# POOL made to wait for the DVE operations planned as sharing its SBUF port, and a weight conversion taken through PSUM, in a fused attention and gated-MLP kernel

## The chip, the cores and the metric

The kernel runs on one core of one Trainium2 chip. The metric is the device time of one execution in microseconds (us). In this text PE is TensorE, DVE is VectorE, ACT is ScalarE, POOL is GpSimd, and SP is the engine whose queue issues most DMAs.

## The reference

An attention block between 512 tokens and 32 states for each of 8 batches and 8 heads (D = 64) gives 4352 rows of 512 values. A gated MLP with 2048 hidden units follows.

```python
scores = scale * x @ state.T          # softmax over the states
xread  = softmax(scores) @ state      # (B, H, 512, 64)
sread  = softmax(scale * state @ x.T) @ x   # (B, H, 32, 64)
y = concatenate([xread, sread], axis=2)     # to (4352, 512)
h = y @ w_in                          # 512 x 2048
g = h * cos(h)
out = g @ w_out                       # 2048 x 512, float32
```

Attention inputs are float32; w_in and w_out come as float64 and are made float32 in the kernel.

## The kernel before

**Tiles.** The token rows are worked on batch by batch, 16 tiles of 128 hidden units each. For a batch, "products" multiplies the states with w_in (state products, result sw_all), so that a hidden tile is one product of the attention weights aT_all with sw_all. A gate follows: ACT rounds (q_all), DVE subtracts, ACT takes a sine, DVE multiplies with h and writes g_all. Output products then take g_all with w_out. Batches 0 and 1 are the first pair and use plain products. From batch 2 on two batches share seven-product block schemes (Strassen's kind) for the hidden tiles ("seven_part", with sums on POOL in sw_sums and on DVE in seven_sum and halves) and for the output products (class Product; its sums of g_all are POOL's, and outer_sum gives more on DVE or POOL). Weight blocks for these are written to device memory (blocks_kept) and fetched into a ring. At the end come the state rows.

**Two lists.** Engines work strictly in the order in which instructions are issued to each. first_pair orders the work of batches 0 and 1 (the first list): each Task has an engine, a cost, what it reads and writes, a due step, and a mark "shares" for a DVE operation that the planner takes to share an SBUF port with POOL. Its instructions all have line L44 in the profile. All later work is first recorded on a tape and then ordered by in_order (the second list, line L1870), with the same kind of planning. In both, a planned lock keeps a sharing DVE operation and a POOL operation from overlapping in the plan; in the running kernel nothing enforced this, unless data did. The planned order of one engine is fixed; between two engines only semaphores for data hold.

**Conversion.** convert(i, p) makes float32 of one piece i of float64 weights (18 pieces, the first four of half size) in five steps: "1" and "2" on ACT (high and low words), "b" on DVE (shift left by three, in place), "c" on DVE (sign bit from the raw words, xor), "d" on POOL (adds the low part). CONV gives the order of pieces 4 to 17, CONV_DUE their due steps. PACE turns a due step into a time, NEAR is how long the planner lets a more urgent task hold the engine, ARRIVED says when the first seven loads are taken to have landed.

**Names.** h_pairs[1] is a pair of PSUM banks ("sd00" to "sd11" in the tasks), used by the state products of the first pair and from batch 2 on by hidden tiles. at is another bank pair, for attention. acc is the pair of output accumulators.

Of the kernel before, what the change touches and what calls it, by code (L numbers as in the profile page):

```python
# [11 lines left out]
I32 = mybir.dt.int32  # L12
# [10 lines left out]
def kernel(  # L23
# [11 lines left out]
    class Lane:  # L35
        def __init__(self, name, engine):
            self.name, self.engine = name, engine

        def __getattr__(self, op):
            f = getattr(self.engine, op)  # L40

            def call(*args, **kw):
                if not taping[0]:
                    return f(*args, **kw)  # L44
                tape.append((self.name, op, f, args, kw, burst[0]))
            return call

    class Lanes:
# [44 lines left out]
    TEMPS = 4  # L93
# [144 lines left out]
    def convert(i, p):  # L238
        if not f64:
            return  # L240
        raw, dst = raws[i], loads[i][0]
        bits = dst.bitcast(I32)
        m, w = dst.shape[1:]
        c0 = m * w if i in (2, 3) else 0
        e = low[i % 2][:, c0:c0 + m * w].rearrange("p (m f) -> p m f", m=m)
        e = e.bitcast(I32)
        if p == "1":
            nc.scalar.activation(dst, raw.bitcast(F32)[:, :, :, 1],
                                 func=ACTF.Abs, scale=2.0 ** -112)
        elif p == "2":  # L250
            nc.scalar.activation(e, raw.bitcast(U32)[:, :, :, 0],
                                 func=ACTF.Copy, scale=2.0 ** -29)
        elif p == "b":
            nc.vector.tensor_scalar(bits, bits, 3, None,
                                    op0=ALU.logical_shift_left)
        elif p == "c":
            nc.vector.scalar_tensor_tensor(out=bits, in0=raw[:, :, :, 1],
                                           scalar=-2 ** 31, in1=bits,
                                           op0=ALU.bitwise_and,
                                           op1=ALU.bitwise_xor)  # L260
        else:
            nc.gpsimd.tensor_tensor(bits, bits, e, op=ALU.add)
# [734 lines left out]
    WARM, START_PE = 8, 19.7  # L997
    ARRIVED = (10.0, 11.3, 12.7, 14.0, 16.6, 19.3, 22.0)

# [165 lines left out]
    def first_pair_tasks():  # L1165
# [10 lines left out]
        def dve(n):  # L1176
            return .06 + n * .00108
# [23 lines left out]
        def conversion(i, due):  # L1201
            n = 512 if i < 4 else 1024
            raw, w, e = raw_of(i), weight_of(i), low_of(i)
            if i > (6 if f64 else 4):
                add("sp", .4, lambda: fetch(i), "", raw, due - 3)
            for p, engine, cost, r, wr, sh in (
                    ("1", "act", act(n) + .05, raw, w, False),
                    ("2", "act", act(n) + .05, raw, e, False),
                    ("b", "dve", n * .0007 + .03, w, w, True),
                    ("c", "dve", dve(n), raw + " " + w, w, True),  # L1210
                    ("d", "pool", pool(n), e + " " + w, w, False)):
                add(engine, cost, lambda p=p: convert(i, p), r, wr, due,
                    sh)

        def attention(b, k):
# [26 lines left out]
            for j in range(2 if b == 0 else 0):  # L1242
                add("act", act(512) + .03,
                    lambda j=j: a.exp1(slice(j, j + 1)), f"z{z}{j}",
                    f"z{z}{j}", k + 4)
            m2 = k + 6 if b == 0 else k + 4
            if b == 0:
# [83 lines left out]
        def tile_(t, k):  # L1331
            n = t.b * NF + t.f
            h, z, c = n % 2, t.b % 2, t.f // 4 % 2
            g = names(quads_of[t.row][t.i // QT], t.i % QT)
            add("pe", 1.72, lambda: hidden(t),
                f"sw{c}{t.f % 4 // 2}0 sw{c}{t.f % 4 // 2}1 z{z}0 z{z}1",
                f"h{h} H", k)
            add("act", act(512) - .04, lambda: gate(t), f"h{h}", f"q{h}")
            add("dve", dve(512) - .02, lambda: gate2(t), f"h{h} q{h}", f"q{h}")
            add("act", .63 if n else 1.91, lambda: gate3(t), f"q{h} T",  # L1340
                f"q{h}")
            add("dve", dve(512) - .02, lambda: gate4(t), f"h{h} q{h}", g,
                k + 2)

# [148 lines left out]
        for step, what in (  # L1493
                (1, lambda: attention_late(0, 0)),
                (3, lambda: products(0, 1, 2.5)),
                (3, lambda: add("pe", .4, lambda: states(1, side_banks[0]),
                                "held0", "sd00 sd01", 8.5)),
                (3, lambda: add("act", .53,
                                lambda: states_kept(1, side_banks[0]),
                                "sd00 sd01", "stT1", 5.5)),  # L1500
                (5, lambda: attention(1, 4)),
                (7, lambda: products(0, 2, 4.5)),
                (11, lambda: products(0, 3, 11.5)),
                (13, lambda: products(1, 0, 16)),
                (13, lambda: attention_late(1, 18)),
                (13, lambda: inner(0, a11, 5, temps[0], names(TEMPS), 14.5)),
                (15, lambda: sends(2, a22, 8, 17)),
                (15, lambda: sums_of(SQ, A21, A22, add_, 16, "pool")),
                (16, lambda: products(1, 1, 18.5)),
                (16, lambda: inner(3, matrix(SQ), SQ, temps[1], E, 17)),  # L1510
                (17, lambda: sums_of(A22, SQ, A11, sub_, 16, "pool")),
                (17, lambda: attention(2, 19)),
                (18, lambda: sums_of(A21, A11, A21, sub_, 20, "dve")),
                (20, lambda: products(1, 2, 23)),
                (20, lambda: inner(5, matrix(A21), A21, temps[0],
                                   names(TEMPS), 20)),
                (20, lambda: sends(1, a12, 6, 22)),
                (21, lambda: inner(4, matrix(A22), A22, temps[1], E, 22)),
                (23, lambda: sums_of(SQ, A12, A22, sub_, 23, "dve")),
                (24, lambda: inner(6, matrix(SQ), SQ, temps[0], names(TEMPS),  # L1520
                                   25)),
                (24, lambda: products(1, 3, 31)),
                (25, lambda: attention_late(2, 25)),
                (24, lambda: [add("sp", .4, lambda n=n: fetch_block(n), "B3",
                                  f"ring{n}", 27) for n in range(NB - 1)])):
            at_step[step].append(what)
        t32, t34 = all_tiles[PERIOD], all_tiles[PERIOD + 2]
        for step, what in (
                (26, lambda: outer(0, 2, 0, 0, 26, "dve")),
                (27, lambda: outer(0, 2, 0, 1, 27, "dve")),  # L1530
                (28, lambda: tokens_of_next(32)),
                (28, lambda: products(2, 0, 28)),
                (28, lambda: p5_tasks(30.5)),
                (29, lambda: weight_columns(t32, 30.5)),
                (29, lambda: add("dve", .7, lambda: halves(2, 0), "z00 z01",
                                 "E0", 30, True)),
                (29, lambda: add("dve", .7, lambda: halves(2, 1),
                                 "z00 z01 E0", "E1", 30, True)),
                (30, lambda: seven_tasks(t32, 29.5)),
                (31, lambda: weight_columns(t34, 32)),  # L1540
# [3 lines left out]
        for step, t in enumerate(all_tiles[0:FIRST]):  # L1544
# [3 lines left out]
            if 4 <= step < 4 + NH:  # L1548
                first(step - 4, step - 1)
            for i in range(NH):  # L1550
                if SECOND_AT[i] == step:
                    second(i, step)
        for what in at_step[FIRST]:
# [3 lines left out]
    SECOND_AT = (16, 17, 19, 20, 22, 24, 26, 27)  # L1557
    CONV = (4, 5, 6, 7, 8, 9, 10, 11, 14, 15, 16, 17, 12, 13)
    CONV_DUE = (3, 4.5, 3.5, 6, 6.7, 8.5, 9, 9.5, 12.0, 11, 11.3, 13.7, 12.5, 15.7)
    PACE, NEAR, SEND = 3.4, 0.3, 2.5  # L1560

# [36 lines left out]
    def first_pair():  # L1598
# [20 lines left out]
        lock = 0.0  # L1619
        cold = True  # L1620
        log = []
        while can:
# [17 lines left out]
            if t.engine == "pe":  # L1640
# [3 lines left out]
                if cold and idle > 0:  # L1644
                    warm(idle, acc[0])
            t.what()
            can.remove(t)
            end = at_ + t.cost
            free[t.engine] = end
            log.append((at_, t))  # L1650
# [125 lines left out]
    def works_of(tape):  # L1776
        works, last, at_ = [], {}, 0.0
        wrote, read = {}, defaultdict(list)
        for engine, op, f, args, kw, n in tape:
            aps = [a for a in list(args) + list(kw.values())  # L1780
# [9 lines left out]
            if not (w is not None and w.burst == n  # L1790
# [6 lines left out]
                if op == "matmul" and kw["lhsT"].partition_size() == D:  # L1797
                    w.cost += .3
            w.calls.append((f, args, kw))
            w.cost += cost_of(engine, op, kw, aps)  # L1800
# [22 lines left out]
    def in_order(tape, free):  # L1823
# [15 lines left out]
        while can:  # L1839
# [20 lines left out]
            for u in after[w]:  # L1860
# [4 lines left out]
                if not waiting[u]:  # L1865
                    can.append(u)
        assert len(log) == len(works)
        for w in sorted(log, key=lambda w: w.start):
            for f, args, kw in w.calls:
                f(*args, **kw)  # L1870

# [74 lines left out]
```

## Time and profile before

| what | value |
|---|---|
| median of 3 runs | 730.56 us (727.94 to 731.85) |
| the profiled execution's own time | 726.99 us |
| its span, first to last instruction | 725.2 us |
| mean granted PE clock | 0.992 |
| PE busy | 701.0 us |
| POOL busy | 540.2 us |
| DVE busy | 508.9 us |
| ACT busy | 348.0 us |
| first instruction of the second list on PE | 157.7 us |

How to read it: a busy PE is not PE at its peak, since the ends of matmuls are modelled. The first list takes 157.7 us and holds 127.4 us of PE busy time after the first 20 us; the second takes 567.5 us with 556.5 us of it busy. Most lines belong to helpers (L44 and L1870), so that instructions are told apart by their tiles.

### The profile page before, as it was taken

To read this page: it belongs to the slowest core of one execution; us is meant where nothing else is said; L and a number is where in the kernel's file an instruction comes from. 1 tells how busy PE (TensorE), PEld (TensorE's weight loads), DVE (VectorE), ACT (ScalarE), POOL (GpSimd) and SP (SyncE) were. 2 spreads that over 40 slices of the span, in tenths; PEclk is the share of its full clock that TensorE was granted. 3 is DMA by queue.
4 is the path that set the end of the run, shared out by engine and by line. 5 is a ranking of instruction groups with operands and counts; after the bars stand their busy time and mean duration, and the time that the engine had idled before them with its cause. 6 is when DMAs were issued, how large, how long until landed. Compare 5 with 4: busy or idle time off the path is not lost.

```text
span 725.2 us, 10728 instructions
## 1 busy us (share of the span) xinstructions
PE 701.0 (97%) x3628; PEld 524.1 (72%) x3628; DVE 508.9 (70%) x698; ACT 348.0 (48%) x591; POOL 540.2 (74%) x524
## 2 busy tenths in 40 slices
PE   8898899999979999999999999999999999999997
PEld 4444344477857878787788787878788888888886
DVE  4899879987876687776986567878766476625630
ACT  5689876754543447444634554445634443211100
POOL 1466799578984998898998856998988848896500
PEclk9999999999989999999999999999999999999999
DMA  9966699756436754783258435762366345465851
GB/s 298 294 194 201 190 260 294 190 137 142 142 82 134 205 130 123 149 193 89 78 128 186 118 88 126 153 147 85 114 153 157 89 111 128 110 200 170 224 103 29
DMA packets 204022, 111.34 MB, mean 154 GB/s; under 512 B 149888, under 2 KB 166784, under 8 KB 203968
## 3 DMA queue, kind: packets, MB, share of 16 engines
q1 hardware_dynamic: 202880, 110.14, 58.5%
q8 instruction: 29, 0.48, 0.3%
q10 hardware_dynamic: 960, 0.39, 0.2%
q14 instruction: 25, 0.20, 0.1%
q0 software_dynamic: 128, 0.13, 0.1%
HBM read 87.03 MB, written 23.59 MB: 153 GB/s over the span
## 4 chain that ended last, share of the span: by engine, by line
PE 67%; DVE 3%; issue 1%; ACT 1%; DVEq 0%
PE o L1870 38%; PE h L1870 21%; PE at L1870 8%; DVE g_all L1870 1%; ACT q_all L1870 1%; DVE q_all L1870 0%; DVE h L1870 0%; DVE xT L1870 0%; DVE aS_all L1870 0%; ACT L1870 0%; DVE aT_all L1870 0%; DVE held L1870 0%; DVE sr L1870 0%; DVE m_all L1870 0%; ACT xT L1870 0%
## 5 line engine op out<-in xcount | busy, mean ns | idle before, releaser
L1870 POOL TENSOR_TENSOR g_all<-g_all 128x512 f32<-128x512 f32 x250 | 329.2, 1344 | 29.2 <-PE o L1870 20.0
L1870 PE MATMUL o<-g_all 128*128 128x256 f32 x1448 | 341.3, 381 | 0.0
L1870 PEld LDWEIGHTS o<-g_all 128*128 128x128 f32 x1448 | 273.5, 191 | 46.8 <-issue 5.6
L1870 ACT ACTIVATE q_all<-h 128x1024 int32<-128x1024 f32 (+1 forms) x56 | 54.1, 965 | 108.3 <-PE h L1870 106.8
L1870 DVE TENSOR_TENSOR q_all<-q_all,h 128x1024 f32<-128x1024 int32 (+1 forms) x56 | 64.0, 1142 | 53.4 <-ACT q_all L1870 53.3
L1870 DVE TENSOR_TENSOR g_all<-h,q_all 128x1024 f32<-128x1024 f32 (+1 forms) x56 | 64.1, 1145 | 28.0 <-ACT q_all L1870 25.6
L1870 ACT ACTIVATE q_all<-q_all,halfpi 128x1024 f32<-128x1024 f32 (+1 forms) x56 | 61.1, 1091 | 26.1 <-DVE q_all L1870 25.8
L44 PE MATMUL h<-aT_all,sw_all 128*128 128x512 f32 (+1 forms) x132 | 62.8, 603 | 5.4 <-DVE g_all L44 5.4
L1870 DVE TENSOR_TENSOR g_all<-g_all 128x1024 f32<-128x1024 f32 (+1 forms) x68 | 67.8, 1039 | 0.1
L1870 DVE TENSOR_TENSOR h<-h,sums_all 128x256 f32<-128x256 f32 x94 | 40.1, 427 | 38.1 <-PE h L1870 33.2
L1870 PE MATMUL h<-aS_all,swS_all 128*128 128x256 f32 x188 | 59.0, 396 | 0.0
L1870 PE MATMUL h<-aS_all,sw_all 128*128 128x256 f32 x188 | 56.3, 381 | 2.7 <-DVE h L1870 2.7
L1870 POOL TENSOR_TENSOR swS_all<-sw_all 128x128 f32<-128x128 f32 x46 | 22.3, 486 | 47.6 <-ACT sw_all L1870 47.3
L1870 PE MATMUL h<-aT_all,sw_all 128*128 128x256 f32 x188 | 56.6, 383 | 0.0
L44 PEld LDWEIGHTS h<-aT_all,sw_all 128*128 128x128 f32 x132 | 23.9, 192 | 36.0 <-issue 21.5
L1870 PEld LDWEIGHTS h<-aS_all,swS_all 128*128 128x128 f32 x188 | 33.9, 191 | 21.3 <-POOL g_all L1870 9.2
L44 POOL TENSOR_TENSOR g_all<-g_all 128x512 f32<-128x512 f32 x30 | 42.2, 1426 | 5.1 <-DVE g_all L44 2.4
L44 PE MATMUL o<-g_all 128*128 128x512 f32 (+1 forms) x112 | 43.7, 520 | 0.0
L44 POOL TENSOR_TENSOR w_in<-w_in,aS_all 128x1024 int32<-128x1024 int32 (+1 forms) x10 | 21.4, 2153 | 29.5 <-DVE w_in L44 22.3
L1870 PEld LDWEIGHTS h<-aS_all,sw_all 128*128 128x128 f32 x188 | 35.2, 190 | 9.0 <-DVE h L1870 3.4
L1870 PEld LDWEIGHTS h<-aT_all,sw_all 128*128 128x128 f32 x188 | 35.8, 192 | 5.5 <-DVE g_all L1870 0.6
L1870 DVE SCALAR_TENSOR_TENSOR held<-o,held 128x512 f32<-128x512 f32 x38 | 26.1, 687 | 12.9 <-PE o L1870 12.3
(159 smaller groups left out, 960.2 us busy)
## 6 DMA issues: line engine op xcount, KB each, us to landing
g_all<-blocks_kept SPq DMA_DIRECT2D x206, 256.0 KB, 2.8
blocks_kept<-g_all SPq DMA_DIRECT2D x48, 256.0 KB, 4.1
g_all<-in_moe_w_out_dram SPq DMA_DIRECT2D x8, 1024.0 KB, 5.5
out_dram<-ot SPq DMA_DIRECT2D x128, 64.0 KB, 2.8
g_all<-in_moe_w_in_dram SPq DMA_DIRECT2D x6, 1024.0 KB, 7.2
x_b<-in_x_dram SPq DMA_DIRECT2D x24, 256.0 KB, 4.6
xT<-in_x_dram SPq DMA_DIRECT2D x80, 64.0 KB, 2.8
x_b<-in_x_dram SPq DMA_DIRECT2D x16, 128.0 KB, 4.1
```

Of the source, the lines that this page charges most:

```text
L44: return f(*args, **kw)
L1870: f(*args, **kw)
```

## The change

Three things are changed.

First, a POOL instruction may be given a wait for a DVE instruction. When the planner of either list issues a POOL operation whose planned start is less than 1.0 us after the planned end of the last sharing DVE operation, that POOL operation gets a semaphore dependency on the last DVE instruction issued so far (Lane.behind; it need not be the sharing one).

Second, from piece 4 on step b of the conversion writes to the PSUM pair h_pairs[1] and step c reads it there. The planner then no longer marks b and c as sharing the port, and takes b at DVE's ordinary cost. The first four pieces stay in place in SBUF, and only for them c stays marked.

Third, the first list has new due steps for nearly all its work, two pieces (10 and 11) swapped, and new planner constants.

```diff
 class Lane:
     def __init__(self, name, engine):
         self.name, self.engine = name, engine
+        self.last = self.behind = None
...
+    def issue(self, f, args, kw):
+        made = self.last = f(*args, **kw)
+        if self.behind is not None:
+            tc.add_manual_dep(made.ins, self.behind.ins.name,
+                              mybir.DependencyInfo(
+                                  mybir.DependencyClass.Sync,
+                                  mybir.DependencyReason.DATA),
+                              reason="ports")
+            self.behind = None
...
+    shifted = bits if i < 4 else h_pairs[1].bitcast(I32)
...
     elif p == "b":
-        nc.vector.tensor_scalar(bits, bits, 3, None,
+        nc.vector.tensor_scalar(shifted, bits, 3, None,
                                 op0=ALU.logical_shift_left)
     elif p == "c":
         nc.vector.scalar_tensor_tensor(out=bits, in0=raw[:, :, :, 1],
-                                       scalar=-2 ** 31, in1=bits,
+                                       scalar=-2 ** 31, in1=shifted,
...
-ARRIVED = (10.0, 11.3, 12.7, 14.0, 16.6, 19.3, 22.0)
+ARRIVED = (10.7, 12.1, 13.5, 14.8, 18.2, 20.9, 23.9)
...
+            x, narrow = (w, True) if i < 4 else ("sd00 sd01 sd10 sd11", False)
+            b_cost = n * .0007 + .03 if narrow else dve(n)
...
-                    ("b", "dve", n * .0007 + .03, w, w, True),
-                    ("c", "dve", dve(n), raw + " " + w, w, True),
+                    ("b", "dve", b_cost, w, x, narrow),
+                    ("c", "dve", dve(n), raw + " " + x, w, narrow),
...
-            add("dve", dve(512) - .02, lambda: gate4(t), f"h{h} q{h}", g, k + 2)
+            add("dve", dve(512) - .02, lambda: gate4(t), f"h{h} q{h}", g, k + 7.5)
...
-                (1, lambda: attention_late(0, 0)),
-                (3, lambda: products(0, 1, 2.5)),
+                (1, lambda: attention_late(0, 3.0)),
+                (3, lambda: products(0, 1, 14.0)),
...
-                first(step - 4, step - 1)
+                first(step - 4, step + 13)
...
-                    second(i, step)
+                    second(i, step + 23.0)
...
-CONV = (4, 5, 6, 7, 8, 9, 10, 11, 14, 15, 16, 17, 12, 13)
-CONV_DUE = (3, 4.5, 3.5, 6, 6.7, 8.5, 9, 9.5, 12.0, 11, 11.3, 13.7, 12.5, 15.7)
-PACE, NEAR, SEND = 3.4, 0.3, 2.5
+CONV = (4, 5, 6, 7, 8, 9, 11, 10, 14, 15, 16, 17, 12, 13)
+CONV_DUE = (1.8, 1.5, 2.1, 5.2, 5.3, 5.2, 10.8, 9.3, 9.7, 11.1, 12.6, 13.2, 13.1, 15.7)
+PACE, NEAR, SEND = 3.6, 0.1, 2.5
...
+            if t.engine == "pool" and dve_end is not None:
+                if at_ < dve_end + 1.0:
+                    pool.behind = dve.last
+                dve_end = None
             t.what()
...
+            if t.engine == "dve" and t.shares:
+                dve_end = end
...
         for w in sorted(log, key=lambda w: w.start):
-            for f, args, kw in w.calls:
-                f(*args, **kw)
+            if w.engine == "pool" and dve_end is not None:
+                if w.start < dve_end + 1.0:
+                    pool.behind = dve.last
+                dve_end = None
+            for lane, f, args, kw in w.calls:
+                lane.issue(f, args, kw)
+            if w.engine == "dve" and w.shares:
+                dve_end = w.start + w.cost
```

No instruction is added or taken away on any engine; only targets of b, waits and the order differ.

## The prediction

> **What bounds the kernel now.** I read four views in this order: the waits of PE, the windows with the granted clock, the timeline of one place, and the groups by form. PE is busy for 701.0 of 725.2 us, so time can only come from its few gaps and from slices in which its clock was low. The first instruction of the second list (L1870) stands on PE at 157.7 us; so I asked for PE's waits before it (first fence) and after it (second fence). Columns: waiting engine, tile and line, what ended the wait, total us, times, longest.
>
> ```profile
> PE h L44 <- DVE g_all L44: 5.4, 5, 1.9
> PE at L44 <- ACT xT L44: 4.3, 4, 2.4
> PE at L44 <- DVE g_all L44: 1.5, 1, 1.5
> ```
>
> ```profile
> PE at L1870 <- ACT xT L1870: 4.4, 1, 4.4
> PE h L1870 <- DVE h L1870: 2.7, 4, 0.9
> ```
>
> The first list loses 13.4 us in waits of PE, half of it (6.9) behind gate products on DVE. In the second list one wait of 4.4 us stands out. The windows around it (us, PE busy, PEld, DVE, ACT, POOL, granted PE clock, DMA share, GB/s) show that it costs more than itself: after it the clock is 0.50 and 0.62.
>
> ```profile
> 208.00:213.00 5.00, 0.65 (x3) 0.22 (x2) 5.00 (x3) 0.59 (x2) 3.24 (x4) 0.92 0.22 52
> 213.00:216.00 3.00, 2.96 (x19) 2.45 (x20) 1.63 (x3) 2.16 (x5) 2.20 (x3) 0.50 0.00 0
> 216.00:220.00 4.00, 4.00 (x13) 3.27 (x12) 2.00 (x3) 1.03 (x1) 1.27 (x1) 0.62 0.41 70
> ```
>
> The timeline names the cause. DVE's normalising product of batch 3 (aT_all<-aT_all,xT) takes 7.12 us, during which POOL runs six sums without a gap; ACT's copy of the turned weights waits for that product, and PE's read for the copy.
>
> ```profile
> 205.21 7.12 DVE L1870 TENSOR_TENSOR aT_all<-aT_all,xT 128x1024 f32<-128x1024 f32 x1
> 205.50 2.48 POOL L1870 TENSOR_TENSOR g_all<-g_all 128x512 f32<-128x512 f32 x2
> 207.94 0.45 POOL L1870 TENSOR_TENSOR swS_all<-sw_all 128x128 f32<-128x128 f32 x1
> 208.35 2.48 POOL L1870 TENSOR_TENSOR g_all<-g_all 128x512 f32<-128x512 f32 x2
> 210.79 0.45 POOL L1870 TENSOR_TENSOR swS_all<-swS_all,sw_all 128x128 f32<-128x128 f32 x1
> 212.41 0.58 ACT L1870 COPY xT<-at 128x512 f32<-128x512 f32 x1 [8.77 <-issue]
> 213.04 1.33 PE L1870 MATMUL at<-x_b,xT 128*64 128x128 f32 x10 [4.40 <-ACT xT L1870]
> ```
>
> The groups by form of DVE between 25 and 110 us price the conversion (busy us, then mean ns; TENSOR_SCALAR is its shift b, SCALAR_TENSOR_TENSOR its step c):
>
> ```profile
> L44 DVE SCALAR_TENSOR_TENSOR g_all<-g_all 128x1024 int32<-128x1024 int32 x8 | 10.2, 1281 | 0.1
> L44 DVE TENSOR_SCALAR g_all<-g_all 128x1024 int32<-128x1024 int32 x8 | 9.1, 1143 | 0.4 <-ACT g_all L44 0.4
> L44 DVE SCALAR_TENSOR_TENSOR w_in<-g_all,w_in 128x1024 int32<-128x1024 int32 x6 | 7.1, 1216 | 0.0
> L44 DVE TENSOR_SCALAR w_in<-w_in 128x1024 int32<-128x1024 int32 x6 | 6.1, 1031 | 0.0
> ```
>
> **What the Trainium skill says.** "SBUF — State Buffer", section "Who interferes with whom": a DVE instruction with two SBUF inputs, or in a two-port mode, and a GpSimd instruction that reads SBUF exclude each other for a whole instruction; one with at most one SBUF input outside those modes does not contend. The trace agrees, and adds that a DVE instruction can lose several times running: 7.12 us above, where the timeline has 1.22 for the same number of elements from PSUM. "VectorE: DVE Perf Modes", section "Why PSUM operands drop a tier": an fp32 operation on one tensor that touches PSUM runs one element per cycle. The trace has b at 0.69 us with both sides in SBUF and no case with PSUM. "TensorE: Matmul & The Clock Gate", Part 1: PE's clock is halved after an idle window of about 3.4 us and comes back after as long of work; the trace agrees (0.50 and 0.62 after 4.4 us).
>
> **The change part by part.** The sum is made against the profiled execution's own 726.99 us (span 725.2 and 1.8 around it), which lies 3.6 below the median of 730.56 and under all three runs.
>
> *Waits of POOL, second list.* The built order gives 43 POOL instructions there a wait for a DVE instruction (and 19 in the first list). At the place above, DVE's normalising product now stands ahead of a gate product (before: behind it), and the POOL sum after both waits for the gate product. POOL cannot then hold the port against the normalising product; the latter waits for one running sum at most (1.27). Gone: the wait, 4.4; the clock, 3.00 x (1 - 0.50) + 4.00 x (1 - 0.62) = 3.0. Next late there is ACT, whose sine ends at 203.64, with two copies of 0.58; the read was due at about 208.4, so nothing of that shows. Of the four waits for DVE h, three (0.56 at 231.0, 0.66 at 355.9, 0.65 at 509.4) come after DVE sums that took 1.42 and 1.49 instead of 0.41, or 2.13 instead of 1.22: 1.9. The fourth, 0.87 at 205.4, stands behind a sine that an ACT table load delays; counted at 0. Together -9.3.
>
> *New cost of these waits.* Behind a waiting POOL sum stand all later POOL sums, and for them PE's products and seven-part blocks. Where POOL's sums are done before PE asks, this is free: no wait of PE itself names POOL in the second list, only its weight loads do (9.2 us in 11, each about 0.8, under cover of running matmuls). Bounds: 0, and 43 x 0.45 (the length of a small sum) = 19. I take 1.0, a few waits of some tenths that reach PE. Covered by POOL's lead; if that is gone, see the second rival.
>
> *Changed start of the second list.* The lists meet at other engine positions, so ACT now runs the exponential burst of batch 3 (1.28 table load + 2.6) ahead of two copies of sums that PE's next product needs; before, the copies stood first. PE has about 3.3 us of other work there, against 3.9: +0.6.
>
> *Conversion through PSUM, first list.* Fourteen shifts b write PSUM. The 1024-wide gate product, which touches PSUM, takes 1.22, so b: 14 x 1.22 = 17.1 against 8 x 1.143 + 6 x 1.031 = 15.3 now. Bounds for one b: 0.69 (no loss from PSUM) and 1.30. c stays at 1.22 and loses 0.5 of collisions. DVE: +1.3 (from -6.2 to +2.4). POOL's step d loses its collisions: means 2.63 (x8) and 2.56 (x6) against 2.34 in undisturbed cases, -3.6 of POOL. The bank pair of b and c also serves the state products: each conversion holds it for about 2.4 us, 14 x 2.4 = 34 us of the 85 between 25 and 110, so those products can wait for it; their new places in PE's order allow for that.
>
> *Own due steps.* The same 93 pieces of PE work and as many warm-up matmuls stand in another order; SP's loads move too: an output-weight load passes an input-weight load, and the twelve token loads of batch 3 go in one run, ahead of ring loads and one store. SP issues are short and no PE wait of the second list names a DMA; if that cover went, one landing (2.8) would show. Both halves of the first state product, and so all four first d, now come ahead of the first tile (before: one half), which can cost about 1 at the start. Of the 13.4 us of waits I assume that a good fifth goes, by POOL's relief and the shorter queues ahead of gate products: -3.0; the views give no closer value. Bounds: all waits behind DVE gates gone, -6.9; as many new ones behind the bank pair, +4.
>
> Sum: -9.3 + 1.0 + 0.6 - 3.0 = -10.7, so 716.3 for a profiled run. The median stood 3.6 higher; locks won by chance may be part of that, so I carry half: 718.
>
> **Rivals.** *Only the one long stall goes.* The first list gains nothing (DVE pays for b what POOL gains) and the small waits return elsewhere: -7.4 + 1.6 = -5.8 on the median, 725. For it: DVE is busy 119.4 of the 137.7 us from 20 to 157.7, so it may set the pace there. Against: half of PE's waits there are behind DVE instructions that collisions pushed back.
>
> *POOL becomes the bound* (slower). From 250 to 350 us POOL is busy 89.75 of 100 and about nine of the waits fall there. Headroom 10.25 / 9 = 1.1 us for each: if a wait costs POOL more than that on average, because the DVE instruction named is itself held by ACT or PE (16 of 43 name one that does not share the port), POOL falls behind. At 1.8 us: 9 x 1.8 - 10.25 = 6 us in each of four such stretches, 24 - 10.7 = +13, so 744. Against: POOL's 435.6 of 567.5 in the whole list leaves room to recover.
>
> *The waits do nothing.* If POOL's winning at 205 was chance that the three timed runs mostly lacked, the gain is in the profile alone: 728 to 731. Against: those runs are slower than the profile, not faster.
>
> **Numbers.** My forecast 718: 0.68. Only the long stall: 0.18. Nothing: 0.06. POOL the bound, or the first list's +4 with it: 0.08. A measurement of this kernel can tell about 0.5% (3.7 us) from no change; faster than that 0.85, within it 0.07, slower 0.08. Range 711 (first list at its best) to 727 (the first rival's end).
>
> **What would show it.** Right: no DVE product over 2.5 us in the second list; no PE wait over 2 us and no clock under 0.9 after 160; b near 1.22 and d near 2.34; PE reaches L1870 near 154.7. Wrong: PE waits naming POOL, POOL idle behind DVE gate products for more than 40 us in all, or L1870 later than 157.7.

## The result, and the profile after

| what | before | after |
|---|---|---|
| median, in the session of the prediction | 731.13 us (4 runs) | 719.59 us (4 runs, 718.96 to 720.12) |
| ratio, with its 95% interval | | 0.9852 (0.9825 to 0.9878) |
| the profiled execution's own time | 726.99 us | 719.58 us |
| its span | 725.2 us | 717.8 us |
| first instruction of the second list on PE | 157.70 us | 158.05 us |
| length of the second list | 567.5 us | 559.75 us |

The kernel is faster by about 1.5% in these runs. The two profiled spans differ by 7.4 us, or 1.0%, and all of that lies in the second list; in three later sessions the kernel before had medians of 727.4 to 728.5, against which 719.59 is 1.1 to 1.2% less. In the kernel after, the lines of both lists are recorded in one helper, so all rows have L51. The waits of PE, first from 20 us to its entry into the second list and then in the second list (waiting engine, tile and line, what ended the wait, total us, times, longest):

```profile
PE h L51 <- DVE g_all L51: 6.0, 5, 1.6
PE h L51 <- DVE i_all L51: 1.9, 1, 1.9
PE h L51 <- ACT sw_all L51: 1.3, 1, 1.3
PE at L51 <- ACT xT L51: 0.8, 2, 0.6
PE h L51 <- POOL w_in L51: 0.3, 1, 0.3
```

```profile
PE h L51 <- DVE h L51: 1.7, 3, 1.3
```

The waits of the first fence sum to 10.3 us, as much as before (5.4 + 3.9 + 0.8 + 0.2 in the same stretch). In the second list the wait of 4.4 us for ACT's copy xT is gone, and with it the cold clock, as the granted clock of 0.50 after it is called here. Windows of the kernel after (us, PE busy, PEld, DVE, ACT, POOL, granted PE clock, DMA share, GB/s):

```profile
207.00:212.00 5.00, 5.00 (x36) 4.08 (x35) 3.42 (x5) 2.82 (x4) 5.00 (x8) 1.00 0.36 88
212.00:216.00 4.00, 4.00 (x31) 3.21 (x30) 3.33 (x7) 0.00 (x0) 4.00 (x5) 1.00 0.79 147
216.00:220.00 4.00, 4.00 (x20) 3.40 (x18) 3.92 (x7) 2.22 (x5) 2.62 (x4) 1.00 0.53 123
```

The timeline of the same place shows how far the remedy reaches. The normalising product still takes 4.62 us, not 1.22. Five POOL sums in a row had begun at 195.86; they and two more were planned ahead of the product and have no wait for it. Only the first sum planned after it, which starts at 205.99, has the wait, and that one is for the gate product. PE waits 1.34 us instead of 4.40.

```profile
195.86 6.19 POOL L51 TENSOR_TENSOR g_all<-g_all 128x512 f32<-128x512 f32 x5
...
200.15 4.62 DVE L51 TENSOR_TENSOR aT_all<-aT_all,xT 128x1024 f32<-128x1024 f32 x1
...
204.70 1.21 DVE L51 TENSOR_TENSOR g_all<-h,q_all 128x1024 f32<-128x1024 f32 x1
204.87 1.07 ACT L51 COPY xT<-at 128x512 f32<-128x512 f32 x2 [4.74 <-DVE aT_all L51]
205.84 0.42 DVE L51 TENSOR_TENSOR h<-h,sums_all 128x256 f32<-128x256 f32 x1
205.99 1.27 POOL L51 TENSOR_TENSOR g_all<-g_all 128x512 f32<-128x512 f32 x1 [2.29 <-DVE g_all L51]
...
206.31 0.70 PE L51 MATMUL h<-aS_all,sw_all 128*128 128x256 f32 x2 [1.34 <-DVE h L51]
```

The conversion, groups by form of DVE between 25 and 110 us (busy us, mean ns): b now writes h, a tile in PSUM, c reads it there, and both stay at 1.22 us (the longest of the 28 took 1.228).

```profile
L51 DVE TENSOR_SCALAR h<-g_all 128x1024 int32<-128x1024 int32 x8 | 9.8, 1223 | 0.9 <-ACT g_all L51 0.8
L51 DVE SCALAR_TENSOR_TENSOR g_all<-g_all,h 128x1024 int32<-128x1024 int32 x8 | 9.7, 1216 | 0.1
L51 DVE TENSOR_SCALAR h<-w_in 128x1024 int32<-128x1024 int32 x6 | 7.3, 1220 | 0.1
L51 DVE SCALAR_TENSOR_TENSOR w_in<-g_all,h 128x1024 int32<-128x1024 int32 x6 | 7.3, 1216 | 0.1
```

One place where the first list loses time is its timeline between 29 and 38 us. ACT's rounding, table load and sine for the first gates stand behind a conversion step that waits 2.32 us for a weight load (piece 7 of the weights):

```profile
31.78 1.16 ACT L51 ACTIVATE w_in<-g_all 128x1024 f32<-128x1024 f32 x1 [2.32 <-DMA g_all<-in_moe_w_in_dram]
...
32.84 0.58 ACT L51 ACTIVATE q_all<-h 128x512 int32<-128x512 f32 x1
...
34.46 1.28 ACT L51 ACT_TABLE_LOAD   x1
...
35.76 0.72 ACT L51 ACTIVATE q_all<-q_all,halfpi 128x512 f32<-128x512 f32 x1
...
36.51 0.69 DVE L51 TENSOR_TENSOR g_all<-h,q_all 128x512 f32<-128x512 f32 x1 [1.80 <-ACT q_all L51]
...
37.26 2.07 PE L51 MATMUL h<-aT_all,sw_all 128*128 128x512 f32 x2 [1.59 <-DVE g_all L51]
```

The windows show what follows: PE is busy for 1.09 of the 3 us from 34 to 37, and its clock is then 0.50.

```profile
34.00:37.00 3.00, 1.09 (x16) 0.21 (x16) 1.16 (x4) 2.97 (x4) 2.15 (x1) 0.97 1.01 337
37.00:40.00 3.00, 2.74 (x4) 1.19 (x5) 2.55 (x7) 2.08 (x4) 0.22 (x1) 0.50 1.35 224
```

### The profile page after: what moved, and what is told of

It reads as the page before. It is cut to its first block, busy times and chain, and to the rows that moved or that the text cites. A ratio compares the mean times of both kernels' runs of the same rounds, so it can differ in the third digit from the quotient of the medians.

```text
span 717.8 us, 10738 instructions
## 1 busy us (share of the span) xinstructions
PE 698.7 (97%) x3628; PEld 522.2 (73%) x3628; DVE 491.6 (68%) x698; ACT 348.7 (49%) x591; POOL 508.3 (71%) x524
## 4 chain that ended last, share of the span: by engine, by line
PE 84%; DVE 6%; ACT 4%; DMA 3%; issue 2%; SPq 0%; ACTq 0%; DVEq 0%
PE o L51 45%; PE h L51 30%; PE at L51 9%; DMA g_all<-in_moe_w_in_dram 2%; DVE g_all L51 2%; DVE h L51 1%; ACT q_all L51 1%; DVE w_in L51 1%; DMA x_b<-in_x_dram 1%; DVE q_all L51 1%; ACT sw_all L51 1%; DMA held<-in_state_dram 0%; ACT aS_all L51 0%; SPq L51 0%; DVE i_all L51 0%
## 5 line engine op out<-in xcount | busy, mean ns | idle before, releaser
L51 POOL TENSOR_TENSOR g_all<-g_all 128x512 f32<-128x512 f32 x280 | 351.1, 1281 | 56.2 <-DVE g_all L51 26.3
L51 PE MATMUL o<-g_all 128*128 128x256 f32 (+1 forms) x1560 | 383.4, 391 | 0.0
L51 PEld LDWEIGHTS o<-g_all 128*128 128x128 f32 x1560 | 293.2, 190 | 64.2 <-issue 22.4
L51 ACT ACTIVATE q_all<-h 128x1024 int32<-128x1024 f32 (+1 forms) x88 | 73.2, 832 | 126.8 <-PE h L51 125.4
L51 DVE TENSOR_TENSOR q_all<-q_all,h 128x1024 f32<-128x1024 int32 (+1 forms) x88 | 85.7, 974 | 67.7 <-ACT q_all L51 67.4
L51 PE MATMUL h<-aT_all,sw_all 128*128 128x256 f32 (+1 forms) x320 | 119.4, 474 | 4.7 <-DVE g_all L51 3.4
L51 DVE TENSOR_TENSOR g_all<-h,q_all 128x1024 f32<-128x1024 f32 (+1 forms) x88 | 85.8, 975 | 35.4 <-ACT q_all L51 34.9
L51 ACT ACTIVATE q_all<-q_all,halfpi 128x1024 f32<-128x1024 f32 (+1 forms) x88 | 84.3, 958 | 31.2 <-DVE q_all L51 30.3
L51 PEld LDWEIGHTS h<-aT_all,sw_all 128*128 128x128 f32 x320 | 59.7, 191 | 40.9 <-issue 20.6
L51 DVE TENSOR_TENSOR g_all<-g_all 128x1024 f32<-128x1024 f32 (+1 forms) x78 | 72.7, 970 | 0.1
L51 DVE TENSOR_TENSOR h<-h,sums_all 128x256 f32<-128x256 f32 x96 | 41.1, 428 | 38.4 <-PE h L51 33.5
L51 PE MATMUL h<-aS_all,swS_all 128*128 128x256 f32 x192 | 59.6, 392 | 0.0
L51 PE MATMUL h<-aS_all,sw_all 128*128 128x256 f32 x192 | 57.6, 381 | 1.7 <-DVE h L51 1.7
L51 POOL TENSOR_TENSOR swS_all<-sw_all 128x128 f32<-128x128 f32 x48 | 21.8, 455 | 43.7 <-ACT sw_all L51 24.5
L51 PEld LDWEIGHTS h<-aS_all,swS_all 128*128 128x128 f32 x192 | 34.5, 189 | 20.5 <-POOL g_all L51 8.4
L51 POOL TENSOR_TENSOR w_in<-w_in,aS_all 128x1024 int32<-128x1024 int32 (+1 forms) x10 | 19.3, 1932 | 33.9 <-DVE w_in L51 28.6
L51 PEld LDWEIGHTS h<-aS_all,sw_all 128*128 128x128 f32 x192 | 36.0, 190 | 8.6 <-DVE h L51 2.3
L51 DVE SCALAR_TENSOR_TENSOR held<-o,held 128x512 f32<-128x512 f32 x38 | 26.1, 686 | 13.7 <-PE o L51 12.9
L51 ACT COPY sw_all<-at 128x512 f32<-128x512 f32 x48 | 25.8, 591 | 16.4 <-PE at L51 16.1
L51 ACT COPY o<-o 128x256 f32<-128x256 f32 x26 | 9.4, 360 | 47.1 <-PE o L51 47.0
L51 ACT COPY o<-sums_all 128x256 f32<-128x256 f32 x26 | 9.7, 375 | 44.9 <-PE o L51 44.9
L51 PE MATMUL h<-st_all,w_in 128*128 128x256 f32 x128 | 30.2, 379 | 0.0
```

The costliest lines, as they stand in the source:

```text
L51: made = self.last = f(*args, **kw)
```

## The experiments

The theory to be tested: the second list's gain comes from POOL's waits, not from the new order that the new start of that list brings; the first list gained nothing because the gates on ACT stand behind the late load of piece 7. The rivals: the new order alone does it; POOL's waits or the pass through PSUM ate the first list's gain; the parts add up one by one. The experiments were run in three sessions of four runs each, in which the kernel before has medians of 727.43, 727.60 and 728.45 us; ratios are against those. "Second list at" gives the time at which PE reaches it in the profiled execution of a run.

### No waits, and waits in the second list only

Both keep every order of the changed kernel. The first switches off the assignment to pool.behind in both planners, the second in first_pair alone:

```diff
-                if at_ < dve_end + 1.0:
+                if False and at_ < dve_end + 1.0:
                     pool.behind = dve.last
```

> The changed kernel with none of the POOL waits for DVE, in either list; every engine's order as in the changed kernel. Theory (the waits, not the new order, end the long loss of the SBUF port in the second list): the normalising product of batch 3 again takes 6 to 7 us instead of 4.62, PE waits 4 us or more there, its clock drops after it, and the small waits at 231, 356 and 509 come back; 724 to 728 us. Rival (the new order is enough, since the normalising product now stands ahead of the gate product): no PE wait over 2 us after 160, 718 to 721 us.

Measured: 729.99 us, ratio 1.0023 (1.0003 to 1.0044). The second list starts at 158.55 and is 568.05 us long: the whole gain is gone. The timeline of the run without waits:

```profile
200.64 10.10 DVE L51 TENSOR_TENSOR aT_all<-aT_all,xT 128x1024 f32<-128x1024 f32 x1
...
203.89 2.51 POOL L51 TENSOR_TENSOR g_all<-g_all 128x512 f32<-128x512 f32 x2
...
206.33 0.48 POOL L51 TENSOR_TENSOR swS_all<-sw_all 128x128 f32<-128x128 f32 x1
206.74 2.51 POOL L51 TENSOR_TENSOR g_all<-g_all 128x512 f32<-128x512 f32 x2
209.18 0.48 POOL L51 TENSOR_TENSOR swS_all<-swS_all,sw_all 128x128 f32<-128x128 f32 x1
210.66 1.21 DVE L51 TENSOR_TENSOR g_all<-h,q_all 128x1024 f32<-128x1024 f32 x1
...
212.27 1.22 PE L51 MATMUL h<-aS_all,sw_all 128*128 128x256 f32 x2 [6.81 <-DVE h L51]
```

The product stands for 10.10 us, until POOL's queue has run empty, and the gate product stands behind it, so that PE waits 6.81 us. The new order without waits is worse at this place than the old one (4.40). Its windows have the cold clock again, 0.50 from 212 to 216:

```profile
212.00:216.00 4.00, 3.73 (x9) 3.02 (x10) 2.36 (x4) 1.76 (x4) 2.09 (x3) 0.50 0.00 0
```

> The changed kernel with the POOL waits in the second list only (the 19 of the first list are left out). Theory (the first list is held up by the late load of weight piece 7, not by POOL's waits): the second list is still reached within 1 us of 158.0, 718.5 to 721 us. Rival (POOL's waits in the first list cost the 3 us that were expected as a gain): second list reached at 155 to 156, 716 to 717 us.

Measured: 721.07 us, ratio 0.9903 (0.9870 to 0.9936); second list reached at 158.54 and 559.82 us long. PE's waits in the second list, without POOL's waits and then with them:

```profile
PE h L51 <- DVE h L51: 8.2, 3, 6.8
```

```profile
PE h L51 <- DVE h L51: 1.7, 3, 1.4
```

The two runs issue the same matmuls in the same order. Set side by side, the second list is shorter by 8.2 us: 5.4 at the long wait, 1.9 in the cold clock after it, and 0.3 to 0.4 net at each of the three small ones. The waits do it, the order does not. What they are worth in the first list can't be told from these starts: 158.54 and 158.55 without them, 158.05 with them.

### The kernel before with the waits alone

The parts of the diff that make pool.behind were put into the kernel before, first in both lists, then in the second only; due steps, constants and conversion stayed as before.

> The kernel before with the POOL waits added in both lists and nothing else (old due steps, conversion in SBUF). Theory (the waits alone give the second list's gain): POOL's sums planned after the normalising product of batch 3 wait for it, it takes under 2.5 us although it still stands behind the gate product, no clock drop at 213; second list 559 to 561 us long, in all 721 to 725 us. Rival (the gain is that of the new order, and the waits without it only make POOL stand): PE waits of 2 us or more stay behind the turned weights' copy, 727 to 732 us.

Measured: 720.68 us, ratio 0.9900 (0.9866 to 0.9933); second list at 159.35, 558.9 us long. In the old order, too, the product is at its undisturbed length, and no wait for the copy remains:

```profile
206.53 0.42 DVE L51 TENSOR_TENSOR h<-h,sums_all 128x256 f32<-128x256 f32 x1
206.86 1.21 DVE L51 TENSOR_TENSOR aT_all<-aT_all,xT 128x1024 f32<-128x1024 f32 x1
```

> The kernel before with POOL's waits in the second list only: its own first list, no PSUM conversion, no new due steps. Theory (the second list's waits are the whole gain of the change; the first list of before is as good as that of the changed kernel): second list reached at 157.7 and 558.9 us long, 717.5 to 719.5 us, not slower than the changed kernel. Rival (the old first list brings the second list into an order, or POOL into a lag, that the waits can't mend): 722 to 727 us.

Measured: 720.10 us (718.99 to 721.62), ratio 0.9891 (0.9867 to 0.9914); second list at 159.61, 558.8 us long. The length came as expected, the start 1.9 us later than the 157.70 of the profile before, with the same first list. So two profiles of one first list can differ by about 2 us. Set matmul beside matmul, 1.7 of the 1.9 us arise between 70 and 74 us. In both profiles PE has waited 1.91 us behind a gate product just before; after it the clock stays at 1.00 in the profile of before and falls to a mean of 0.57 in this run:

```profile
70.00:74.00 4.00, 4.00 (x11) 1.71 (x9) 3.93 (x7) 4.00 (x6) 0.10 (x1) 1.00 0.12 45
```

```profile
70.00:74.00 4.00, 4.00 (x7) 1.54 (x5) 3.93 (x7) 3.62 (x5) 0.02 (x1) 0.57 0.17 66
```

The waits alone reach what the whole change reaches, within what can be told apart; in one session, the kernel before with the waits in both lists has 720.68, and the changed kernel with those of the second list 721.07. The rest of the change is worth nothing that these runs can show.

### The conversion in place, with the new order kept

```diff
-        shifted = bits if i < 4 else h_pairs[1].bitcast(I32)
+        shifted = bits
```

The planner still takes b and c as not sharing the port, so nothing keeps them from POOL.

> The changed kernel with step b of pieces 4 to 17 again in place in SBUF and c reading it there; all engine orders and the planner's claims on the bank pair kept. Theory (the pass through PSUM neither makes nor breaks the first list): b back at about 1.1 us instead of 1.23, POOL's d back at 2.5 to 2.6 instead of 2.37, second list reached at 157.5 to 159.5, 719 to 721 us. Rival (holding the bank pair and the slower b eat the expected gain): second list reached at 155 to 156, 716 to 717 us.

Measured: 727.26 us, ratio 0.9994 (0.9976 to 1.0013); second list only at 163.76. Both expectations missed: with this order, in which nothing keeps b and c from POOL, the second list starts 5.7 us later without PSUM (6.2 between the medians of this run and of the one with waits in the second list only). The timeline shows the mechanism, c against POOL's step d:

```profile
60.94 2.67 POOL L51 TENSOR_TENSOR w_in<-w_in,aS_all 128x1024 int32<-128x1024 int32 x1 [1.23 <-DVE w_in L51]
61.43 3.27 DVE L51 SCALAR_TENSOR_TENSOR g_all<-g_all 128x1024 int32<-128x1024 int32 x1
64.62 0.68 DVE L51 TENSOR_TENSOR g_all<-h,q_all 128x512 f32<-128x512 f32 x1
...
65.35 2.05 PE L51 MATMUL h<-aT_all,sw_all 128*128 128x512 f32 x3 [3.18 <-DVE g_all L51]
```

Here c has both inputs in SBUF and takes 3.27 us instead of 1.22; the gate product stands behind it, and PE waits 3.18 us. Over the 14 pieces b and c cost 15.4 + 12.0 + 9.9 + 6.4 = 43.7 us of DVE, against 9.8 + 9.7 + 7.3 + 7.3 = 34.1 with PSUM. This agrees with the Trainium skill, "SBUF — State Buffer", section "Who interferes with whom": with one input in PSUM, c has one SBUF input left and does not contend.

### One of the two other parts at a time, planned anew

The first kernel is the one before with waits and PSUM; the second is the changed kernel with the conversion in SBUF and marked as sharing. In both the planner orders the first list anew.

> The kernel before with the POOL waits and with step b of the conversion through PSUM, but with the old due steps and constants; the planner orders the first list anew for it. Theory (PSUM conversion and new due steps only work together, since the conversion now claims the bank pair of the state products, and the old due steps leave no room for that): second list reached later than in the kernel before with waits alone (159.35), at 163 to 171, and 724 to 732 us. Rival (the parts add up one by one): 157 to 159.5 and 718 to 721 us.

Measured: 732.57 us, ratio 1.0056 (1.0034 to 1.0078); second list at 172.39. PE's waits behind gate products sum to 10.3 us from 20 us on, against 6.0 in the changed kernel, and its mean clock from 80 to 100 us is 0.74.

> The changed kernel (waits, new due steps and constants) with the conversion kept in SBUF and marked as sharing the port, as before; the planner orders the first list anew. Theory (as for the run with PSUM and old due steps: the parts work only together): second list reached at 163 to 171, 724 to 732 us. Rival (the new due steps are good by themselves, and PSUM is not needed): 156 to 159 and 717 to 720 us.

Measured: 728.93 us, ratio 1.0012 (0.9991 to 1.0034); second list at 169.02. The second lists are 559.4 and 560.0 us long, so the waits work in both; each gives their gain back in the first list. The due steps and the bank pair as a buffer belong together: with one of them alone the second list starts 13.0 and 9.7 us later than with neither (159.35), and both together come to where the old pair was. The old due steps with PSUM did worse than the 171 us expected. Which resource makes them late was not taken apart further; that it is the bank pair, as the expectation says, is not shown, nor how much lies in the order that the planner found anew.

### The late load of piece 7

One number of the planner: the second of the large loads is taken to land later, so that ACT's rounding and sine stand ahead of the step that waits for it.

```diff
...
                 end = lanes - 1.8
+                n_loads += size > 1
+                if n_loads == 2:
+                    end = 33.0 - SEND
```

> The changed kernel with one number of the planner changed: piece 7's load is taken to arrive so late that ACT's rounding and sine of the first gates stand ahead of the conversion step that waits for it (in the changed kernel ACT stands for that load for 2.32 us at 29.5 with the gate behind it, PE then waits 1.85 and 1.59 us, and its clock falls to 0.74). Theory (that stand is what ate the gain expected of the first list): both PE waits at 34 to 38 are gone, no clock under 0.9 from 34 to 40, second list reached at 154.5 to 156.5, 716 to 718 us. Rival (DVE, busy without a gap from 26 to 35, sets the pace there, and any gain is lost again in the later waits behind gate products): second list reached at 157 to 159.5, 719 to 721 us.

Measured: 717.88 us (715.98 to 718.46), ratio 0.9846 (0.9821 to 0.9871); second list at 155.76, 2.3 us ahead of the changed kernel's 158.05 (and 3.2 ahead of 158.97 in the next run, which shares its session and has the changed kernel's order). The profiled execution, 716.11, is one of the two fastest here, 1.8 below the median. The sine stands at 33.87 instead of 35.76, and the gate product directly behind it:

```profile
33.87 0.72 ACT L51 ACTIVATE q_all<-q_all,halfpi 128x512 f32<-128x512 f32 x1
34.25 0.16 DVE L51 TENSOR_SCALAR i_all<-i_all 128x2 f32<-128x2 f32 x1
34.44 0.17 DVE L51 RECIPROCAL i_all<-i_all 128x2 f32<-128x2 f32 x1
34.48 1.09 PE L51 MATMUL h<-w_in,st_all 64*32 64x512 f32 x16 [1.85 <-DVE i_all L51]
34.49 1.30 ACT L51 ACTIVATE w_in<-g_all 128x1024 f32<-128x1024 f32 x1
34.62 0.69 DVE L51 TENSOR_TENSOR g_all<-h,q_all 128x512 f32<-128x512 f32 x1
```

Of the two PE waits that were expected to go, the one of 1.59 us went, and with it the cold clock (1.00 from 37 to 40). The other, 1.85 us, stayed: it hangs on DVE, which has no gap from 26 to 35 us in either kernel. Both theories have a part: moving ACT's gates ahead of the late load takes the 1.59 us wait away, and DVE's pace holds what is left. How much of this reaches the second list is less sure than 2.3 us, as the last two runs below show. PE's waits behind gate products from 20 us on fell from 6.0 to 3.6. The second list is shorter too (558.5), since the normalising product met fewer POOL sums and took 1.76 us.

### What the wait names

Both lists get this edit; that of the second is shown.

```diff
...
-                    pool.behind = dve.last
+                    pool.behind = sharing
...
             if w.engine == "dve" and w.shares:
-                dve_end = w.start + w.cost
+                dve_end, sharing = w.start + w.cost, dve.last
```

> The changed kernel with each POOL wait naming the sharing DVE operation itself, instead of the last DVE instruction issued so far. Theory (the gain lies in holding POOL back from the sharing operation alone, and POOL has room for the longer waits): no measurable difference, 718.5 to 721 us, second list again 559 to 561 us long. Rival (naming a later DVE instruction, itself held by ACT, costs POOL time that reaches PE): 716.5 to 718 us.

Measured: 718.86 us (717.76 to 719.31), ratio 0.9865 (0.9842 to 0.9887); second list at 158.97 and 558.25 us long. The second list lost 1.5 us against the changed kernel, nearly all of it at the wait of 1.34 us: the product took 3.16 us in this run, and the gate product came early enough. A product of 3.16 beside one of 4.62 is a matter of how far POOL lags, and the run with the late load lost the same wait without this edit; so it is not shown that the name did it. The first list was 0.9 us later, within the spread of profiles; PE's clock was at half for 6.8 us of it, against 3.4 us in the changed kernel. The median can't be told from the changed kernel's.

### One wait, and two combinations

> The changed kernel with one wait only in the second list, that of the POOL sum planned after the normalising product of batch 3; the waits of the first list are kept. Theory (nearly all of the second list's gain is that one stall with its cold clock; the other 42 waits only take away three small PE waits): second list 560.5 to 562.5 us long, against 559.75 with all 43 and 568.05 with none; 720 to 722.5 us. Rival (the 42 others count for more, since POOL loses or gains ground over many sums): 563 to 567 us long, 723 to 727 us.

The edit keeps a wait of the second list only where POOL's planned start lies between 202 and 203 us. Measured: 729.50 us, ratio 1.0011 (0.9997 to 1.0025); second list 567.8 us long. The run doesn't answer its question: the wait that was kept stands behind another normalising product, at about 360 us, since it had been picked by a time that counts from the start of the second list. At 202.5 the product of batch 3 has no wait behind it and takes 10.04 us. What follows is only that a wait elsewhere does not help there.

> The changed kernel with the later planned arrival of piece 7 (as in the run with that alone) and, in the second list, each POOL wait naming the sharing operation itself. If both gains are independent (2.3 us in the first list, 1.5 in the second): second list reached at 155.8 and 558.2 us long, 715.5 to 717.5 us. If the second list's 1.5 is the small PE wait at 204.6, which is gone already with the later arrival: the same as with that alone, 717 to 718.5 us.

Measured: 716.56 us (714.84 to 718.66), ratio 0.9833 (0.9807 to 0.9858); second list at 158.23 and 558.7 us long. The second list is no shorter than with the later arrival alone, so the gain there was the same one wait. Its start compares with 160.40 in the run with one wait, which has the changed kernel's first list and was measured in the same session: again 2.2 us, though ACT's first conversion step starts at 10.87 in the one and at 11.75 in the other, which may explain some of it. The cold clock from 37 to 40 us, gone with the later arrival alone, is back here (0.50). The profiled execution is the slowest of the six, 718.66.

> As the run with both, but without any POOL wait in the first list. Theory (in the first list the waits are worth about half a us, as between the changed kernel at 158.05 and its run without waits at 158.55): second list reached at 155.8 to 157, 716 to 718.5 us. Rival (the first list's waits hold POOL back where its step d is needed): reached at 154.5 to 155.5, 714.5 to 716 us.

Measured: 718.68 us (718.12 to 719.72), ratio 0.9869 (0.9845 to 0.9893); second list at 158.48. Whether the first list's waits are worth anything beside the later arrival stays open: the starts say 0.25 us (158.23 with them), the medians of the two runs 2.1 us (716.56 with them).

What the later arrival itself is worth is not settled either. Like should be set beside like, for PE's clock is at half for 3.4 us of the first list (after 20 us) in some profiles and for 6.8 in others. With 3.4 us, the second list starts at 155.76 with the later arrival and at 158.05 in the changed kernel; with 6.8 us, at 158.23 and (without the first list's waits) 158.48 with it, and at 158.97 and 160.40 in the two runs that have the changed kernel's first order. So it is ahead by 0.5 to 2.3 us, and the medians of one session, 717.88 and 718.86, are 1.0 us apart with intervals that overlap. The run with both edits has the lowest median, but its interval overlaps the changed kernel's; the waits of the second list are sure, the rest is about the size of the spread.

## Why the prediction was right, and where not

The forecast was 718 us, the median 719.59.

**The second list was right in size and cause.** Both kernels issue its matmuls in the same order, but for a stretch between 193 and 200 us, so their starts can be set side by side:

| step of the sum | predicted | measured |
|---|---|---|
| exponential burst ahead of two copies | +0.6 | +0.2 by 205 us |
| wait for DVE h at 205.4 | 0 | +0.4 |
| wait for the copy at 213.0 | -4.4 | -4.5 |
| cold clock after it | -3.0 | -2.8 |
| waits at 231.0, 355.9 and 509.4 | -1.9 | -0.8, -0.8, -0.7 |
| new cost of POOL's waits | +1.0 | none seen |
| new starts late, after the last two of these | 0 | +0.9 |
| sum | -7.7 | -8.0 to the last matmul, -7.75 to the end of the span |

The +0.9 is two places, 0.45 each, about 8 us after the second and third of the small waits. There PE waits for an h sum behind a gate product, and that for a sine behind a table load (1.28 us), which the wait before it used to hide. The 1.0 for POOL's waits had the right size for another reason: no PE wait of the second list names POOL.

**Two tells failed.** PE reached the second list at 158.05, not near 154.7, and a start later than 157.7 had been named as a sign of being wrong; the next paragraph is about it. And the product was to take under 2.5 us and took 4.62. The step that failed there is "the latter waits for one running sum at most (1.27)": it holds only for sums that are planned after the product, and those planned before it, still queued because POOL lags, win as before. The step's time was right all the same: the gate product and the h sum behind it were 0.4 us later than before, where 0 was counted.

**The first list failed.** Predicted was -3.0, measured +0.35. The step that failed is "a good fifth goes, by POOL's relief and the shorter queues ahead of gate products". POOL's relief came (d at 2.37 us against 2.6, b at 1.22 as worked out), but the waits behind gate products summed to 6.0 us from 20 us on, where 5.4 had been (with the 1.5 us wait ahead of that, 7.5 against the 6.9 that the prediction counted; all waits of the first list summed to 13.1 in the profile before, not 13.4). What the prediction treated as free, the passing of one load by another, came with ACT's gates behind a late load: 2.32 us of ACT's wait, 1.59 of PE's, and a cold clock after it. With ACT's order mended the second list starts 0.5 to 2.3 us earlier between profiles that have the same time at half clock, so that this place is a part of the missing 3.3 us; how large a part stays open. The bound of +4 had been put on the bank pair alone; each part alone, the bank pair or the new due steps, starts the second list some 10 us or more later, so that -3.0 was a guess at the small remainder of parts that do not add up one by one.

**The carry.** 1.7 us were added to the sum because the median of before stood above its profile. Later sessions put that median at 727.4 to 728.5, close to the profile's 726.99. So for the profiled run the sum said 716.3 and 719.58 came; the carry covered half of the first list's miss by luck.

**The rivals.** That only the long stall goes was right on the first list, which gained nothing, and half right on the small waits, of which 0.9 of 2.3 came back elsewhere; it went wrong in the sum, 725, since the second list alone brought 7.75 and not 5.8. POOL did not become the bound: from 160 us on its waits for what DVE writes to g_all, the gate products among it, sum to 29.6 us (20.0 + 9.6), under the 40 named. Behind DVE in all POOL waits some 74 us there, against 24 before, and still no wait of PE in the second list names POOL. That the waits do nothing is refuted by the run without them.

## What to carry to other kernels

Where two engines lock each other out of a port, do not trust that an order planned without overlap is kept: here the planned lock held nothing back, and a product of 1.2 us took 7.12. Give the less urgent engine a semaphore wait, and count as its cost only what is queued behind it. Such a wait holds back what is issued later; it can't recall what is already queued, so look at how far that engine lags its plan. And when a load changes place in a queue, follow it to the in-order engine that waits for it and to all that stands behind that wait there.

## What was not expected of the hardware

- A DVE product with both inputs in SBUF does not take its turn after one POOL instruction. It waited for the sum that was running and six more in the kernel before (7.12 us), and for eleven, six long and five short, in the kernel without waits (10.10 us), until POOL's queue had a gap, against 1.21 us undisturbed.
- Step c with one operand in PSUM escaped this: it took 1.216 us on average and 1.221 at most, but up to 3.28 with both in SBUF.
- The same wait of PE can cost only itself or much more. After 1.91 us of waiting the clock stayed at 1.00 in one profile and was at half from 70.2 to 73.6 us in another, with the same instructions; that cost 1.7 us. The wait is shorter than the 3.4 us or so of idling that the prediction names as the condition. So a start that moves by 2 us between single profiles shows little.
- First landings differ between executions: ACT's first conversion step, which waits for the first weight load, started between 10.04 and 11.75 us. With the changed kernel's first list 10.07 went with a second list at 158.05 and 11.75 with 160.40; but with the old one, starts of 157.70 and 159.61 went with 10.41 and 10.23, so this does not explain the spread.
